# Turns of two token blocks, state products in one row, and diagonals on ScalarE, in a linear-attention kernel with two layers behind it

## The chip, the cores and the metric

The kernel runs on one core of a Trainium2 chip. The metric is the device time of that core in microseconds. Three timed runs and one profiled execution of the kernel before are at hand.

## The reference

First a linear attention with a decaying state, 4 sequences of 768 tokens, 8 heads of 48 channels; then two layers of width 384 - 2048 - 384 over the 3072 tokens:

```python
for t in range(S):
    cur = np.einsum('bhd,bhe->bhde', u[None] * kt, vt)
    y[:, :, t] = np.einsum('bhd,bhde->bhe', rt, state + cur)
    state = w[None, :, :, None] * state + np.einsum('bhd,bhe->bhde', kt, vt)
...
h = x @ w_in
sp = np.where(h > 20.0, h, np.log1p(np.exp(np.minimum(h, 20.0))))
x = (h * np.tanh(sp)) @ w_out
...
h = x @ w_in
P = a[0] + a[1] * h + a[2] * h2 + a[3] * h3
Q = 1.0 + np.abs(b[0]) * np.abs(h) + np.abs(b[1]) * h2
out = (P / (Q + 1e-06)) @ w_out
```

## The kernel before, in words

The attention is cut into 24 units. Unit U handles 128 tokens (chunk c of 6) of one sequence (b of 4), all 8 heads: c, b = divmod(U, 4). The function `unit` (L614) loads k, r (both transposed), and k, v in token order, scales them by powers of w, and makes one 128 by 128 score block for each head: row `sc` (L641). Two tiles `am` of four heads each are first written as diagonals (`diag`, L652: a mask times the column `dg`; on VectorE or GpSimd one instruction, L655, on ScalarE four, L658), then a predicated copy from PSUM puts the scores beside the diagonal (L663). `values` (L669) multiplies by the values (L673) and, where c is not 0, by the state of this sequence (L678), into one PSUM bank `pv`: for each pair of heads first the two products with values, then the two with the state. In the profile each such fp32 matmul is two records, so a unit has 16 records at L673 and 16 at L678. `kv` (L698) makes the chunk's own k-v products, which L707 to L712 add to the state. The result goes through SBUF and two DMAs (xr) and is split into a high and a low fp32r part, xh and xl (`split`, L476), 128 columns of the 512 of block c. xh and xl have two buffers each (L536), y and xr two, am four.

The two layers work on blocks of 512 tokens: block (l, c) is layer l, chunk c, and holds the four units of chunk c. A block is 16 steps, f = 0 to 15, one for each 128 of the 2048 inner columns. A step (`step`, L758) has nine matmuls g1 (L772: three times three products of high and low parts), the activation, a split of its result into gh and gl, and nine matmuls g2 (L848) that add into three PSUM banks `acc`, one buffer each (L742). In layer 0 the activation is one VectorE instruction (L787), four on ScalarE (L791), one on VectorE (L793); the split is a copy (mostly ScalarE) and a subtraction on VectorE (L797). At a block's end the three sums are scaled by -2, copied to SBUF and stored to `x2d` in HBM, where layer 1 reads them.

The list `steps` (L485 to L491) sets the order of the blocks. Block (0, 0) is done in half steps of 256 columns: half 0 of step i, then half 1 of step i - 2; half 0 needs units 0 and 1, half 1 units 2 and 3. All other blocks follow one by one in full steps of 512 columns. `weights(0, f)` (L724) loads one step's weights of layer 0 (768 KB) and turns the 64-bit numbers into two fp32r parts: one scaling on ScalarE or GpSimd, three integer instructions on VectorE (L64, L67, L71), a copy for the high part and a subtraction for the low part (L481).

The order on every engine is fixed at build time by a planner (`Plan.order`): each operation has one cost for each engine that may run it, a due time worked out back from the end, and a boost that makes it earlier. Units with c of 1 or more have boost AHEAD = 40 (L612). The cost of a VectorE option can carry an extra: `PV` = 0.0 (L467) for products of the units with c below 2 and the weights of layer 0, and 3.0 for all later ones. Before the first step, matmuls of zeros (L837, L841) fill gaps on TensorE; they open the accumulators of block (0, 0).

```python
    lag = 2
    steps = []
    for i in range(NF + lag):
        steps += [((0, 0), f, p) for f, p in ((i, 0), (i - lag, 1)) if 0 <= f < NF]
    for blk in blocks[1:]:
        steps += [(blk, f, None) for f in range(NF)]
```

Of the kernel before, what the change touches and what calls it, by code (L numbers as in the profile page):

```python
# [12 lines left out]
ALU = mybir.AluOpType  # L13
# [4 lines left out]
B, H, S, D = 4, 8, 768, 48  # L18
DM, DFF = 384, 2048
CH = 128  # L20
NC = S // CH
NF = DFF // 128
# [373 lines left out]
def tt(n):  # L396
    return 0.07 + 1.04e-3 * n
# [18 lines left out]
def fast_path(tc, nc, d):  # L416
    ctx, es1 = ExitStack(), ExitStack()
    V, A, G, T, SP = "V", "A", "G", "T", "S"
    eng = {V: nc.vector, A: nc.scalar, G: nc.gpsimd, T: nc.tensor, SP: nc.sync}
    pl = Plan()  # L420
# [26 lines left out]
    def fixed(p, name, shape, dt=F32):  # L447
        t = p.tile(shape, dt, name=name)
        b = Buf(None, lambda: t)
        return b  # L450

    def bc(x, n):
        return x[:, :, None].to_broadcast([x.shape[0], x.shape[1], n])

    def dma(dst, src, r=(), w=(), nbytes=196608, after=(), boost=0.0):

        return pl.add([(SP, 0.65 if nbytes == 98304 else 0.5)], lambda e: nc.sync.dma_start(out=dst(), in_=src()),
                      r=r, w=w, lat=0.757, after=after, move=nbytes / 3.6e5, boost=boost)
# [5 lines left out]
            return nc.gpsimd.tensor_scalar(out=out, in0=x, scalar1=1.0, scalar2=0.0, op0=ALU.mult, op1=ALU.add)  # L464
        return nc.vector.tensor_copy(out, x)

    PV = 0.0  # L467

    def hi_opts(n):
        return [(A, act(n)), (V, ts(n), True, 3.0), (G, pts(n))]  # L470
# [11 lines left out]
                      r=r + [w[0]], w=[w[1]], boost=boost, what=what)  # L482


    blocks = [(l, c) for l in range(2) for c in range(NC)]  # L485
    lag = 2
    steps = []
    for i in range(NF + lag):
        steps += [((0, 0), f, p) for f, p in ((i, 0), (i - lag, 1)) if 0 <= f < NF]
    for blk in blocks[1:]:  # L490
        steps += [(blk, f, None) for f in range(NF)]  # L491


    fin = cst.tile([1, 1], I32, name="fin")
# [14 lines left out]
    dmk = fixed(att, "dmk", [CH, CH])  # L509
# [99 lines left out]
                                              ps()[:, 0:192].rearrange("p (j e) -> p j e", j=4)),  # L609
                   r=[ps], w=[(P_t, i)])  # L610

    AHEAD = 40.0  # L612

    def unit(U):  # L614
        c, b = divmod(U, B)
        last = U >= NU - B
        bo = AHEAD if c else 0.0
        kraw, rraw, tkv, tr, dg = n_kraw(), n_rraw(), n_tkv(), n_tr(), n_dg()
        st = state[b]
        dma(kraw, lambda: d["kT"][c, b], boost=bo, w=[kraw], nbytes=262144)  # L620
# [30 lines left out]
        for i in range(2):  # L651
            def diag(e, i=i):  # L652
                dgi = dg().rearrange("p (j c) -> p c j", c=2)[:, i]
                if e != A:
                    return eng[e].tensor_tensor(out=am[i](), in0=dmk()[:, None, :].to_broadcast([CH, 4, CH]),  # L655
                                                in1=bc(dgi, CH), op=ALU.mult)
                for j in range(4):
                    x_ = nc.scalar.activation(out=am[i]()[:, j, :], in_=dmk(), func=AF.Copy, scale=dgi[:, j:j + 1])  # L658
                return x_
            pl.add([(G, 1.3), (V, tt(512), True, PV if c < 2 else 3.0), (A, 1.5)], diag, r=[dg, dmk], w=[am[i]], boost=bo)  # L660
        for i in range(2):
            pl.add([(V, tt(512))],
                   lambda e, i=i: nc.vector.copy_predicated(  # L663
# [3 lines left out]
        pv, y, xr = n_ps(), n_y(), n_xr()  # L667

        def values(e):  # L669
            for j in range(4):  # L670
                for i in range(2):
                    h = 2 * j + i
                    x_ = nc.tensor.matmul(pv()[64 * i:64 * i + D, j * CH:(j + 1) * CH],  # L673
                                          lhsT=tkv()[:, 384 + h * D:384 + (h + 1) * D], rhs=am[i]()[:, j, :],
                                          start=True, stop=(c == 0))
                for i in range(2 if c else 0):
                    rows = slice(64 * i, 64 * i + D)
                    x_ = nc.tensor.matmul(pv()[64 * i:64 * i + D, j * CH:(j + 1) * CH],  # L678
                                          lhsT=st()[rows, j * D:(j + 1) * D], rhs=rraw()[rows, j, :],
                                          start=False, stop=True)  # L680
            return x_
        pl.add([(T, 2.4 if c else 1.2)], values, r=[tkv, rraw] + ([st] if c else []) + am, w=[pv], boost=bo,
               rows=0.8)
        pl.add([(A, act(512, 0.052)), (V, tt(512))],
               lambda e: copy(e, y()[:, :, :CH], pv().rearrange("p (h t) -> p h t", h=4)), r=[pv], w=[y], boost=bo)
# [70 lines left out]


    def step(s, after):  # L758
        blk, f, half = steps[s]
        l, cb = blk  # L760
        n = 512 if half is None else 256
        col = 256 * (half or 0)
# [36 lines left out]
        else:  # L799
# [28 lines left out]
                   lambda e: nc.vector.scalar_tensor_tensor(out=g(), in0=g(), scalar=cf()[:, 0:1], in1=h(),  # L828
                                                            op0=ALU.add, op1=ALU.mult), r=[h, cf], w=[g])
            split(n, g, ghs, gls, g, (gh, gl))  # L830
        if f == 0 and not half:
            acc[blk] = [x() for x in n_acc]
            if half == 0:

                def zeros(e):
                    for a in acc[blk]:
                        x_ = nc.tensor.matmul(a(), lhsT=zer(), rhs=zer()[:, None, :].to_broadcast([CH, 4, CH]),  # L837
                                              start=True, stop=False)
                    return x_
                pl.filler = pl.add([(T, 0.64)], zeros, r=[zer], w=acc[blk])  # L840
                pl.fill = lambda e, a=acc[blk][0]: nc.tensor.matmul(  # L841
                    a(), lhsT=zer(), rhs=zer()[:, None, :].to_broadcast([CH, 4, CH]), start=False, stop=False)
        ac = acc[blk]

        def g2(e, ms=range(3)):
            for m in ms:
                for i, (a, x) in enumerate(((0, gh), (0, gl), (1, gh))):
                    x_ = nc.tensor.matmul(ac[m]()[:, col:col + n], lhsT=w()[:, a, 3 + m, :], rhs=x()[:, :n],  # L848
                                          start=(f == 0 and i == 0 and half is None),
                                          stop=(f == NF - 1 and i == 2 and half != 0))  # L850
            return x_
        last = s == len(steps) - 1
        if not last:
            follow(1, pl.add([(T, 9 * mm)], g2, r=rw + [gh, gl], w=[(a, 0) for a in ac], what="g2"), 18 * mm)
        if f == NF - 1 and half != 0:
            for m in range(3):
                if last:
                    y = pl.add([(T, 3 * mm)], lambda e, m=m: g2(e, [m]), r=rw + [gh, gl], w=[ac[m]], what="g2")
                    if m == 0:
                        follow(1, y, 18 * mm)  # L860
                o = n_o()

                def put(e, m=m, o=o):
                    if l:
                        return copy(e, o(), ac[m]())
                    if e == A:
                        return nc.scalar.activation(out=o(), in_=ac[m](), func=AF.Copy, scale=-2.0)
                    return nc.vector.tensor_scalar(out=o(), in0=ac[m](), scalar1=-2.0, scalar2=None, op0=ALU.mult)
                pl.add([(A, act(512, 0.052)), (V, tt(512))], put, r=[ac[m]], w=[o], boost=8.0)
                if l == 0:  # L870
                    dma(lambda m=m: x2d[cb]()[:, m, :], o, r=[o], w=[(x2d[cb], m)], nbytes=262144)
                else:
                    dma(lambda m=m: d["out"][cb, :, m, :], o, r=[o], nbytes=262144)
# [26 lines left out]
        weights(0, f)  # L900

    nu = 2
    for s, (blk, f, half) in enumerate(steps):
        need = 0 if blk[0] else B * (blk[1] + 1) if half is None else 2 * half + 2
        while nu < NU and nu < need:
            end = unit(nu)
            nu += 1
        if blk == (0, NC - 1) and f >= 1:
            weights(1, f - 1)
        if blk == (1, 0) and f == 0:  # L910
            weights(1, NF - 1)
        nxt = blocks.index(blk) + 1
        if f == 12 and half != 0 and nxt < len(blocks) and blocks[nxt][0] == 1:
            x2(blocks[nxt][1])
        step(s, [end])
    with tc.manual_schedule():
# [81 lines left out]
```

## Time and profile before

| what | value |
|---|---|
| timed runs | 979.3, 978.96, 970.26 us; median 978.96 |
| profiled execution, own time | 970.99 us |
| its span, first to last instruction | 969.3 us |
| mean granted clock of TensorE | 0.976 |
| busy: TensorE, VectorE, ScalarE, GpSimd | 930.1, 715.6, 727.3, 500.1 us |

The profile is one execution. Busy time of TensorE comes from records that overlap, since matmuls are pipelined: the distance from one start to the next tells more than a record's own length. A granted clock of 1.00 is 2.4 GHz, 0.50 is 1.2 GHz, and a stretch with both shows a mean.

### The profile page before, as it was taken

The page shows a single profiled execution, that of the slowest core. Times are in us where ns is not written, and L with a number is a line of the kernel's source. Part 1 is how long each engine was busy: PE and PEld are TensorE (multiplying, and loading weights), DVE is VectorE, ACT ScalarE, POOL GpSimd, SP SyncE. Part 2 cuts the span into 40 slices and gives each one's busy share as a digit, 9 for nine tenths or more (in the row PEclk, how much of TensorE's full clock was granted, in tenths as well). Part 3 has the DMA queues.
Part 4 walks back from the last instruction along what each step waited for, and adds up shares of the span by engine and source line. Part 5 has one row for each costly group of instructions (what it writes and reads, how often), then busy time and mean ns, then how long its engine had stood idle before and what let it go on. Part 6 is the DMA issues. An engine that isn't in the chain of part 4 may idle for free. (4 is left out here: it accounts for less than half of the span.)

```text
span 969.3 us, 14361 instructions
## 1 busy us (share of the span) xinstructions
PE 930.1 (96%) x5186; PEld 745.8 (77%) x5186; DVE 715.6 (74%) x1120; ACT 727.3 (75%) x1290; POOL 500.1 (52%) x441
## 2 busy tenths in 40 slices
PE   6798999999999999999999999999999999999995
PEld 4576788788778668767888878888888888888883
DVE  8999898874544544544458998888888788878883
ACT  2465776777677657666777998997988888979784
POOL 1345366420340560051037488786777786877673
PEclk7698999999999999999999999999999999999999
DMA  8765565300320350140025510010020100100001
GB/s 294 245 196 157 170 190 174 109 20 1 104 57 1 97 153 2 28 127 24 0 72 179 169 59 11 1 66 1 1 66 0 55 12 1 55 1 1 32 1 36
DMA packets 36848, 71.98 MB, mean 74 GB/s; under 512 B 4129, under 2 KB 16546, under 8 KB 36770
## 3 DMA queue, kind: packets, MB, share of 16 engines
q1 hardware_dynamic: 36770, 71.00, 23.2%
q8 instruction: 42, 0.69, 0.3%
q14 instruction: 36, 0.29, 0.1%
HBM read 56.83 MB, written 9.44 MB: 68 GB/s over the span
## 5 line engine op out<-in xcount | busy, mean ns | idle before, releaser
L848 PE MATMUL acc<-gh,w 128*128 128x512 f32 (+1 forms) x1248 | 391.5, 375 | 1.4 <-ACT gh L462 1.3
L772 PE MATMUL h<-xh,w 128*128 128x512 f32 (+1 forms) x1020 | 323.0, 377 | 11.5 <-DVE w L481 4.4
L791 ACT ACTIVATE e<-e 128x512 f32<-128x512 f32 (+1 forms) x448 | 250.7, 568 | 52.7 <-DVE e L787 44.2
L848 PEld LDWEIGHTS acc<-gh,w 128*128 128x128 f32 x1248 | 229.6, 188 | 45.8 <-ACT gh L462 2.8
L848 PE MATMUL acc<-gl,w 128*128 128x512 f32 (+1 forms) x624 | 233.4, 374 | 2.7 <-POOL gl L481 1.7
L772 PEld LDWEIGHTS h<-xh,w 128*128 128x128 f32 x1020 | 189.7, 191 | 50.4 <-DVE w L481 5.2
L772 PE MATMUL h<-xl,w 128*128 128x512 f32 (+1 forms) x510 | 190.2, 373 | 0.7 <-POOL xl L481 0.7
L481 POOL TENSOR_TENSOR gl<-yy,gh 128x512 fp32r<-128x512 f32 x96 | 125.4, 1308 | 46.5 <-ACT gh L462 31.5
L810 POOL TENSOR_TENSOR v<-v,x 128x512 f32<-128x512 f32 x96 | 124.9, 1304 | 32.5 <-ACT v L804 17.5
L848 PEld LDWEIGHTS acc<-gl,w 128*128 128x128 f32 x624 | 117.5, 188 | 24.8 <-POOL gl L481 2.7
L793 DVE SCALAR_TENSOR_TENSOR h<-e,h 128x512 f32<-128x512 f32 (+1 forms) x112 | 68.8, 615 | 81.9 <-ACT e L791 81.5
L772 PEld LDWEIGHTS h<-xl,w 128*128 128x128 f32 x510 | 97.7, 192 | 16.7 <-POOL xl L481 0.9
L787 DVE TENSOR_SCALAR e<-h 128x512 f32<-128x512 f32 (+1 forms) x112 | 68.4, 610 | 47.7 <-PE h L772 47.4
L462 ACT ACTIVATE gh<-h 128x512 fp32r<-128x512 f32 (+1 forms) x97 | 53.0, 547 | 59.0 <-DVE h L793 58.6
L812 ACT ACTIVATE x<-v,ceps 128x512 f32<-128x512 f32 x96 | 69.4, 723 | 17.5 <-POOL v L810 17.3
L797 DVE TENSOR_TENSOR gl<-h,gh 128x512 fp32r<-128x512 f32 (+1 forms) x112 | 68.4, 610 | 13.5 <-ACT gh L462 10.6
L804 ACT ACTIVATE v<-x,cf 128x512 f32<-128x512 f32 x96 | 78.2, 815 | 0.0
L772 PE MATMUL aps<-xh,w 128*128 128x512 f32 x228 | 76.3, 392 | 0.0
L712 POOL TENSOR_TENSOR st<-st,pw 128x192 f32<-128x192 f32 x16 | 9.2, 573 | 109.3 <-DVE st L710 109.3
L822 DVE SCALAR_TENSOR_TENSOR v<-v,ceps,h 128x512 f32<-128x512 f32 x58 | 43.2, 746 | 24.0 <-ACT h L820 23.8
L673 PE MATMUL aps<-am,tkv 128*48 128x128 f32 x384 | 45.2, 320 | 7.7 <-DVE am L663 7.7
L481 POOL TENSOR_TENSOR w<-wr,w 128x768 fp32r<-128x768 f32 x18 | 34.9, 1940 | 30.0 <-ACT w L462 29.4
(104 smaller groups left out, 1353.8 us busy)
## 6 DMA issues: line engine op xcount, KB each, us to landing
wr<-in_w SPq DMA_DIRECT2D x32, 768.0 KB, 4.4
tkv<-in_tkv SPq DMA_DIRECT2D x24, 384.0 KB, 3.5
kraw<-in_kT SPq DMA_DIRECT2D x24, 256.0 KB, 3.1
rraw<-in_rT SPq DMA_DIRECT2D x24, 256.0 KB, 2.9
tr<-in_tr SPq DMA_DIRECT2D x24, 192.0 KB, 2.4
xr<-y SPq DMA_DIRECT2D x48, 96.0 KB, 3.2
x<-o SPq DMA_DIRECT2D x18, 256.0 KB, 2.4
o<-x SPq DMA_DIRECT2D x18, 256.0 KB, 2.8
```

The source lines that it names most:

```text
L462: return nc.scalar.activation(out=out, in_=x, func=AF.Copy)
L481: lambda e: eng[e].tensor_tensor(out=lo(), in0=x(), in1=hi().bitcast(F32), op=ALU.subtract),
L673: x_ = nc.tensor.matmul(pv()[64 * i:64 * i + D, j * CH:(j + 1) * CH], lhsT=tkv()[:, 384 + h * D:384 + (h + 1) * D], rhs=am[i]()[:, j, :], ...
L772: x_ = nc.tensor.matmul(h()[:, :n], lhsT=w()[:, a, m, :], rhs=x()[:, m, col:col + n], start=(i == 0), stop=(i == 8))
L787: pl.add([(V, tt(n))], lambda e: nc.vector.tensor_scalar(out=es(), in0=hp(), scalar1=20.0, scalar2=None, op0=ALU.min), r=[h], w=[e_])
L791: lambda e, func=func, kw=kw: nc.scalar.activation(out=es(), in_=es(), func=func, **kw), w=[e_])
L793: lambda e: nc.vector.scalar_tensor_tensor(out=hp(), in0=es(), scalar=-0.5, in1=hp(), op0=ALU.add, op1=ALU.mult), r=[e_], w=[h])
L797: lambda e: nc.vector.tensor_tensor(out=gls(), in0=hp(), in1=ghs().bitcast(F32), op=ALU.subtract),
L804: lambda e: nc.scalar.activation(out=v(), in_=x(), func=AF.Identity, scale=cf()[:, 5:6], bias=cf()[:, 4:5]), r=[x, cf], w=[v])
L810: lambda e: eng[e].tensor_tensor(out=v(), in0=v(), in1=x(), op=ALU.mult), r=[x], w=[v])
L812: lambda e: nc.scalar.activation(out=x(), in_=v(), func=AF.Ln, bias=ceps()), r=[v, ceps], w=[x])
L848: x_ = nc.tensor.matmul(ac[m]()[:, col:col + n], lhsT=w()[:, a, 3 + m, :], rhs=x()[:, :n], start=(f == 0 and i == 0 and half is None), sto ...
```

## The change

1. Order of blocks. Blocks (0, 0) and (0, 1) take turns: (0, 0) f 0 to 7, (0, 1) f 0 to 7, (0, 0) f 8 to 15, (0, 1) f 8 to 15. Only the first six steps of the first turn are in halves, all of half 0 first. Since there is one set of accumulators, a turn's sums leave: the first turn's as at any block's end, and at the end of a block's second turn the stored sums are loaded again, added on VectorE (`if f0:`) and stored.
2. Units with c = 1 have boost 10 in place of 40; the others keep theirs.
3. `values`: all eight state products first, in one row, then all eight with the values.
4. `diag`: VectorE is no longer an option; ScalarE (cost 1.2 in place of 1.5) or GpSimd. PV is 0.3 in place of 0.0.

```diff
+    TURNS, HALVES = 2, 6
...
-    PV = 0.0
+    PV = 0.3
...
-    lag = 2
     steps = []
-    for i in range(NF + lag):
-        steps += [((0, 0), f, p) for f, p in ((i, 0), (i - lag, 1)) if 0 <= f < NF]
-    for blk in blocks[1:]:
-        steps += [(blk, f, None) for f in range(NF)]
+    for blk, f0, f1 in [(blocks[i % 2], NF // TURNS * (i // 2), NF // TURNS * (i // 2 + 1)) for i in range(2 * TURNS)] + \
+            [(blk, 0, NF) for blk in blocks[2:]]:
+        turn = [(f, None) for f in range(f0, f1)]
+        if not steps:
+            turn = [(f, i) for i in range(2) for f in range(HALVES)] + turn[HALVES:]
+        steps += [(blk, f, half, k == 0, k == len(turn) - 1, f0) for k, (f, half) in enumerate(turn)]
...
-    AHEAD = 40.0
+    AHEAD, AHEAD1 = 40.0, 10.0
...
-        bo = AHEAD if c else 0.0
+        bo = AHEAD if c > 1 else AHEAD1 if c else 0.0
...
-            pl.add([(G, 1.3), (V, tt(512), True, PV if c < 2 else 3.0), (A, 1.5)], diag, r=[dg, dmk], w=[am[i]], boost=bo)
+            pl.add([(A, 1.2), (G, 1.3)], diag, r=[dg, dmk], w=[am[i]], boost=bo)
...
         def values(e):
+            for j in range(4 if c else 0):
+                for i in range(2):
+                    rows = slice(64 * i, 64 * i + D)
+                    x_ = nc.tensor.matmul(pv()[64 * i:64 * i + D, j * CH:(j + 1) * CH],
+                                          lhsT=st()[rows, j * D:(j + 1) * D], rhs=rraw()[rows, j, :],
+                                          start=(j == 0), stop=False)
             for j in range(4):
                 for i in range(2):
                     h = 2 * j + i
                     x_ = nc.tensor.matmul(pv()[64 * i:64 * i + D, j * CH:(j + 1) * CH],
                                           lhsT=tkv()[:, 384 + h * D:384 + (h + 1) * D], rhs=am[i]()[:, j, :],
-                                          start=True, stop=(c == 0))
-                for i in range(2 if c else 0):
...
+                                          start=(j == 0 and c == 0), stop=(j == 3))
...
-        pl.add([(T, 2.4 if c else 1.2)], values, r=[tkv, rraw] + ([st] if c else []) + am, w=[pv], boost=bo,
+        pl.add([(T, 2.1 if c else 1.1)], values, r=[tkv, rraw] + ([st] if c else []) + am, w=[pv], boost=bo,
...
-        if f == NF - 1 and half != 0:
+        if final:
...
+                if f0:
+                    dma(o, lambda m=m: x2d[cb]()[:, m, :], r=[(x2d[cb], m)], w=[o], nbytes=262144, boost=20.0)
+                    pl.add([(V, tt(512) + 0.06)],
+                           lambda e, m=m, o=o: nc.vector.scalar_tensor_tensor(
+                               out=o(), in0=ac[m](), scalar=-2.0, in1=o(), op0=ALU.mult, op1=ALU.add),
+                           r=[ac[m]], w=[o], boost=8.0)
+                    dma(lambda m=m: x2d[cb]()[:, m, :], o, r=[o], w=[(x2d[cb], m)], nbytes=262144)
+                    continue
```

## Rows read from the trace of the kernel before

**Rows 1.** Stretches: busy us (records) of PE, PEld, DVE, ACT, POOL; clock, DMA share, GB/s.
```profile
0.00:37.84 37.84, 24.55 (x179) 18.67 (x179) 31.50 (x65) 11.70 (x17) 9.87 (x17) 0.73 0.87 292
37.84:100.00 62.16, 54.84 (x474) 42.50 (x474) 58.94 (x101) 38.12 (x94) 25.10 (x22) 0.83 0.59 176
100.00:176.75 76.75, 71.29 (x687) 59.25 (x686) 68.36 (x129) 54.73 (x137) 45.58 (x44) 1.00 0.55 173
176.75:251.50 74.75, 74.75 (x367) 61.86 (x365) 48.87 (x74) 56.27 (x96) 12.22 (x11) 1.00 0.11 33
...
500.00:961.70 461.70, 456.20 (x1995) 374.73 (x1993) 386.88 (x567) 395.78 (x650) 338.08 (x280) 1.00 0.12 41
```

**Rows 2.** The same view, line 673 on TensorE (products with values) alone.
```profile
0.00:37.84 37.84, 7.07 (x48) 0.73 0.87 292
37.84:100.00 62.16, 10.64 (x80) 0.83 0.59 176
100.00:176.75 76.75, 8.80 (x80) 1.00 0.55 173
```

**Rows 3.** Timeline of TensorE, one unit in steady state: start, us, instructions.
```profile
251.65 0.43 PE L673 MATMUL aps<-am,tkv 128*48 128x128 f32 x4
252.01 0.42 PE L678 MATMUL aps<-rraw,st 48*48 48x128 f32 x4
...
254.49 0.56 PE L698 MATMUL aps<-tkv 128*48 128x48 f32 x16
...
257.25 1.16 PE L641 MATMUL aps<-rraw,kraw 48*128 48x128 f32 x16
258.34 0.50 PE L848 MATMUL acc<-gh,w 128*128 128x512 f32 x1
```

**Rows 4.** Timeline of TensorE at half clock, values and state of a unit.
```profile
92.72 0.67 PE L673 MATMUL aps<-am,tkv 128*48 128x128 f32 x4
93.32 0.67 PE L678 MATMUL aps<-rraw,st 48*48 48x128 f32 x4
```

**Rows 5.** Timeline of weight loads at half clock, a unit without state.
```profile
46.49 1.51 PEld L673 LDWEIGHTS aps<-am,tkv 128*48 128x48 f32 x14 [0.40 <-issue]
```

**Rows 6.** Timeline of TensorE, half-width and full-width matmuls.
```profile
165.59 0.28 PE L772 MATMUL h<-xh,w 128*128 128x256 f32 x1
...
168.71 0.28 PE L772 MATMUL h<-xh,w 128*128 128x256 f32 x1
...
186.28 0.39 PE L848 MATMUL acc<-gh,w 128*128 128x512 f32 x1
...
188.32 0.39 PE L772 MATMUL h<-xh,w 128*128 128x512 f32 x1
```

**Rows 7.** Groups of VectorE's instructions, 0 to 179 us: count, busy us, mean ns.
```profile
L67 DVE SCALAR_TENSOR_TENSOR wr<-wr 128x768 int32<-128x768 int32 x17 | 19.0, 1115 | 0.0
...
L71 DVE SCALAR_TENSOR_TENSOR wr<-wr 128x768 int32<-128x768 int32 x16 | 16.6, 1037 | 0.0
L481 DVE TENSOR_TENSOR w<-wr,w 128x768 fp32r<-128x768 f32 x14 | 16.3, 1167 | 0.7 <-ACT w L462 0.7
...
L787 DVE TENSOR_SCALAR e<-h 128x256 f32<-128x256 f32 x32 | 13.3, 415 | 4.6 <-PE h L772 4.5
L64 DVE TENSOR_SCALAR wr<-wr 128x768 int32<-128x768 int32 x17 | 11.8, 704 | 0.0
L655 DVE TENSOR_TENSOR am<-dmk,dg 128x512 f32<-128x512 f32 x13 | 10.5, 823 | 0.1
```

**Rows 8.** Timeline of ScalarE: one diagonal tile, four instructions.
```profile
87.51 1.26 ACT L658 ACTIVATE am<-dmk,dg 128x128 f32<-128x128 f32 x4
```

**Rows 9.** Waits of TensorE, 0 to 175 us: total, times, longest.
```profile
PE aps L673 <- DVE am L663: 7.7, 3, 4.4
```

**Rows 10.** Groups by form, whole run: an evacuation on VectorE.
```profile
L868 DVE TENSOR_SCALAR o<-acc 128x512 f32<-128x512 f32 x7 | 4.8, 685 | 0.7 <-PE acc L848 0.7
```

**Rows 11.** Waits of all engines, whole run.
```profile
POOL xh L464 <- PE h L772: 39.6, 1, 39.6
```

More of the change, by code (lines that the diff above doesn't have):

```diff
@@ L674, in values @@
                                           lhsT=tkv()[:, 384 + h * D:384 + (h + 1) * D], rhs=am[i]()[:, j, :],
-                                          start=True, stop=(c == 0))
-                for i in range(2 if c else 0):
[L677 to L680, printed above, removed]
+                                          start=(j == 0 and c == 0), stop=(j == 3))
             return x_
-        pl.add([(T, 2.4 if c else 1.2)], values, r=[tkv, rraw] + ([st] if c else []) + am, w=[pv], boost=bo,
+        pl.add([(T, 2.1 if c else 1.1)], values, r=[tkv, rraw] + ([st] if c else []) + am, w=[pv], boost=bo,
                rows=0.8)
@@ L758, in step @@
     def step(s, after):
-        blk, f, half = steps[s]
+        blk, f, half, first, final, f0 = steps[s]
         l, cb = blk
@@ L830, in step, with zeros @@
             split(n, g, ghs, gls, g, (gh, gl))
-        if f == 0 and not half:
+        if first:
             acc[blk] = [x() for x in n_acc]
-            if half == 0:
-                def zeros(e):
-                    for a in acc[blk]:
+            if s == 0:
+                def zeros(e, first=acc[blk]):
+                    for a in first:
                         x_ = nc.tensor.matmul(a(), lhsT=zer(), rhs=zer()[:, None, :].to_broadcast([CH, 4, CH]),
@@ L848, in g2 @@
                     x_ = nc.tensor.matmul(ac[m]()[:, col:col + n], lhsT=w()[:, a, 3 + m, :], rhs=x()[:, :n],
-                                          start=(f == 0 and i == 0 and half is None),
-                                          stop=(f == NF - 1 and i == 2 and half != 0))
+                                          start=(first and i == 0 and s > 0), stop=(final and i == 2))
             return x_
@@ L902, in fast_path @@
     nu = 2
-    for s, (blk, f, half) in enumerate(steps):
+    for s, (blk, f, half, *_) in enumerate(steps):
         need = 0 if blk[0] else B * (blk[1] + 1) if half is None else 2 * half + 2
@@ L912, in fast_path @@
         nxt = blocks.index(blk) + 1
-        if f == 12 and half != 0 and nxt < len(blocks) and blocks[nxt][0] == 1:
+        if f == 12 and nxt < len(blocks) and blocks[nxt][0] == 1:
             x2(blocks[nxt][1])
```

## The prediction

> **What bounds the kernel now.** I read the share of each engine by stretch first [rows 1]. From 176.75 to 251.5 us TensorE is busy in all of the time at full granted clock, and from 500 to 961.7 in 456.2 of 461.7 us: there the time is TensorE's own work, and only less of that work, or an earlier start of it, shortens the run. Before 176.75 us it is otherwise. VectorE is busy for 31.50 of 37.84, 58.94 of 62.16 and 68.36 of 76.75 us, ScalarE and GpSimd for clearly less, and TensorE has gaps and a granted clock of 0.73 and 0.83 in the first two stretches (a mean between its two levels). The one wait of TensorE that stands out there is the products with the values waiting for am from VectorE [rows 9].
>
> How much is lost before 186.28 us, where the first 512-wide g2 starts? Spacing comes from the timeline [rows 6]: a 256-wide matmul takes (168.71 - 165.59) / 26 = 0.120 us, a 512-wide one (188.32 - 186.28) / 9 = 0.2267 us. Until 186.28 TensorE has done block (0,0), 576 x 0.120 = 69.1 us, and three g1 of block (0,1), 27 x 0.2267 = 6.1. It has also done the values of 13 units (48 + 80 + 80 = 208 records, 16 for each unit [rows 2]), nine of them with a state. A unit at full clock costs [rows 3]: 254.49 - 251.65 = 2.84 us for values and state, 258.34 - 257.25 = 1.09 for scores, and the k-v products' row takes 0.56. Values without state I take as one row like the scores, 1.1. That is 13 x 1.09 + 9 x 2.84 + 4 x 1.1 + 12 x 0.56 = 50.9 us, and some 38 changes between kinds of rows, estimated at 0.11 us, add 4. Sum 130.1, so 56.2 us of the first 186.28 are lost, 30 of them before the first g1 at 37.84. That is what the order of the first blocks can give back; nearly nothing can be given back later.
>
> The values of 13 units by 176.75 us also say that all of c = 1 and c = 2 were made while block (0,0), which needs only units 0 to 3, was still running. VectorE spent its scarce time on work not yet due.
>
> **The change, part by part. Rows of products.** Now a unit's values and state alternate in groups of four records, a group every 0.354 us (252.01 - 251.65) [rows 3], though the records inside a group follow closely: the row of 16 score records with the same halves of the array takes 1.09, change to the next kind included. At half clock the trace has both forms: the alternating groups are 93.32 - 92.72 = 0.60 us apart [rows 4], and 14 weight loads of values alone take 1.51 us, with an estimated 0.2 for the last one's own length, so about 0.10 each and 0.40 for four [rows 5]. So the alternation, not the arithmetic, costs 0.2 us a group there. At full clock the two new rows cost at most 2 x 1.09 = 2.18 us (the score row loads 128 columns, these load 48), and at least 2 x 16 x 0.05 + 2 x 0.13 = 1.9, half the half-clock spacing plus two changes. The saving is 0.66 to 0.94 us, in no case shown below zero; I take 0.66, the nearest row. 20 units have a state: 13.2 us, up to 19. All of them run where TensorE is or becomes the bound, so nothing hides the saving.
>
> The Trainium skill, page "TensorE: Matmul & The Clock Gate", section "Wait — 56ns, not 53.3ns?", says that without hardware decode a matmul occupies the sequencer for about 62 ns; two rows would then cost 2 x 16 x 0.062 + 0.26 = 2.24 us, and the saving would be 12 us, an estimate from that page. The k-v row here speaks against that floor, 16 records in 0.56 us, 0.035 each [rows 3].
>
> **Fewer half-width steps.** 32 half steps become 12 and ten full steps: 10 x 18 x (2 x 0.120 - 0.2267) = 2.4 us saved.
>
> **Turns.** The first turn (block (0,0), f 0 to 7) needs units 0 to 3 and eight weights in place of sixteen; units with c = 1 have a boost of 10 in place of 40. I sum VectorE, the binding engine. A weight costs 0.70 + 1.12 + 1.04 + 1.17 = 4.0 us on it [rows 7], a half step 3 x 0.415 = 1.25, a full step at 0.69 each 2.07 (the width of the evacuation in [rows 10]). All 158.8 us of VectorE up to 176.75 [rows 1] less 63.7 for weights, 43 for the steps (3 x 13.3 and some copies), 10.5 for diagonals and an estimated 6 for constants leave 35.6 for 13 units, 2.7 each; with the tail of contention I take 3. First turn: 4 x 3 + 8 x 4.0 + 12 x 1.25 + 2 x 2.07 + 6 = 69 us, and VectorE idled 9.6 us in the first 100, so it ends at about 79. TensorE's work by then is 12 x 2.16 + 2 x 4.08 + 4 x 2.7 + 1.5 = 46.4, so 33 us are lost. Second turn: TensorE 8 x 4.08 + 4 units of 3.8 = 48 us, VectorE 8 x 2.07 + 4 x 3 = 29: TensorE binds, and VectorE has 19 us for the weights of the third turn. Third: VectorE 8 x 6.1 = 49 less those 19, TensorE 33 to 48. So it binds no more; I allow 5 us for places where order is worse than the sum. Loss 38 in place of 56.2: 18 us saved, between 0 (nothing of it comes) and 28 (TensorE busy from 37.84 on).
>
> **Diagonals.** Thirteen leave VectorE, 10.5 us [rows 7], for ScalarE at 4 x 0.316 = 1.26 us each [rows 8] or GpSimd. This is in the sum of the turns (units at 3 us, without them). ScalarE has room: 38.12 of 62.16 us and 54.73 of 76.75 busy [rows 1]. Without that room it would cost TensorE's wait for am again, 1.26 - 0.8 a tile, 16 x 0.5 = 8 us at most over the first eight units. PV 0.3 moves some early products to GpSimd in the same way, where half of the time is free; I take 0, between -3 and +3.
>
> The Trainium skill, page "ScalarE: Activation LUTs", section "Rules for kernel authors", tells to keep plain multiplies on VectorE. The rows agree as to the single instruction (1.26 against 0.82); by that rule the chain of each unit grows and those 8 us come on top, giving about 948 in the profile. VectorE's load of 95% decides against it, I think.
>
> **Turnover.** Two more turn ends: three sums leave for HBM, come back and are added on VectorE, 0.69 us each [rows 10]. The loads are early and the next turn's g1 (2.04 us each, three banks) cover the evacuation; I take 1 us for each added end, 2 in all, 0 to 6.
>
> **Sum.** -13.2 - 2.4 - 18 + 2 = -31.6 us, from the profiled execution's 970.99 us (span 969.3) to 939.4. The three other times known are 970.26, 978.96 and 979.3, so the median shown lies 8 us above the profiled execution; the middle of all four is some 4 us above it, and I set the forecast at 944.
>
> **Rivals.** (1) Only TensorE's own savings come. VectorE stays the bound through all four turns because the same weights, units and steps are still due, or the third turn starves for weights 8 to 15. For: its total hardly falls. Against: blocks (0,0) and (0,1) with twelve units need 6 + 16 x 4 + 12 x 1.25 + 26 x 2.07 + 12 x 3 = 175 us of it, and TensorE needs some 207 by then. Gain 13.2 + 2.4 - 2: 957 in the profile, 961 as forecast. (2) More comes: first g1 earlier, a denser first turn, rows at 1.9 us. -19 - 2.4 - 26 + 2: 926 to 930. (3) The rows don't become cheaper, as both add into the same bank and each product must wait for the one before. Against it the half-clock row [rows 5]. Then -20 + 2: 953 to 957. (4) Slower: x has two buffers, so the x of block (0,2) can be written only after the last g1 of the third turn. Before there was a whole block of 65 us behind that point, now half a block, 33 us. For: GpSimd stood 39.6 us before such a write [rows 11]. y and xr have two buffers as well, so if all four units queue behind that point, they come two by two; I estimate 23 us for a pair, from the 37.84 us that the first pair took with constants and first loads. 2 x 23 = 46 us of chain, and were none of it covered, 939 + 46 = 985. It decides against the change from 32 us of stall on. Against: two units can be ready up to the write, and 33 us cover the other pair.
>
> **How the numbers follow.** Forecast 0.62 (its own range 930 to 955), rival (1) 0.18, (2) 0.11, (3) 0.05, (4) 0.04. Low 922 takes in rival (2); high 964 takes in (1) and its 8 us of scatter; about 0.15 is left out. About 1% is what can be told from no change. Faster by over 1%: forecast, (2), (3) and two thirds of (1), 0.90; within 1%: the rest of (1), 0.06; slower: 0.04.
>
> **What would show it.** Right: values and state of a unit as two rows, scores-like, 2.2 us or less to the next row; TensorE busy throughout from about 80 us; no diagonals on VectorE; c = 2 units after 115 us. Wrong: groups as far apart as now; waits of g1 for w after 115 us; waits of g1 for xh or xl at the start of block (0,2); TensorE waiting for accumulators at turn ends.

## The result, and the profile after

| | before | after |
|---|---|---|
| median, us (four runs each) | 974.97 | 946.13 |
| range, us | 970.26 to 979.3 | 943.59 to 946.39 |
| profiled execution, its span, us | 970.99, 969.3 | 946.39, 944.4 |
| mean granted clock | 0.976 | 0.977 |
| first sums leave, us (before: block (0,0); after: its first turn) | 183.8 | 117.5 |
| first Abs of layer 1 on ScalarE, us | 560.6 | 537.2 |

The ratio is 0.9699, 95% interval 0.9637 to 0.9762: faster by 3%. The forecast of 944 is 2 us off. By profiled executions, which is how the sum was made, it is 946.39 against 939.4: 24.6 us gained in place of 31.6, at nearly the same mean granted clock. By medians it is 28.8 us, since the profile of before was one of its faster executions and that of after the slowest of its four. Of the 24.6, 23.4 are there when layer 1 begins, so nearly the whole effect arises ahead of it.

The sum was 7 us too high and its parts were further off than that, as the following views show. First the timeline of TensorE after, at a unit of the first turn and at the end of the second turn; the columns are as in [rows 3], L679 is the row with the state, L685 the one with the values, L705 the k-v row, L779 is g1 and L855 g2.

```profile
69.95 1.08 PE L679 MATMUL aps<-rraw,st 48*48 48x128 f32 x16
70.96 1.08 PE L685 MATMUL aps<-am,tkv 128*48 128x128 f32 x16
71.87 0.53 PE L705 MATMUL aps<-tkv 128*48 128x48 f32 x16
...
155.39 0.39 PE L855 MATMUL acc<-gh,w 128*128 128x512 f32 x1
155.71 1.08 PE L679 MATMUL aps<-rraw,st 48*48 48x128 f32 x16
156.72 1.08 PE L685 MATMUL aps<-am,tkv 128*48 128x128 f32 x16
157.73 0.50 PE L779 MATMUL h<-xh,w 128*128 128x512 f32 x1
```

A unit's two rows now take 71.87 - 69.95 = 1.92 us up to the k-v row, where they took 2.84 [rows 3]: 0.92 saved. The sixteen records of values take 0.91, 0.057 each on the average. The last four rows are the end of the second turn: from the last g2 to the first g1 of the third turn TensorE does only the two rows of a unit, and nothing waits for an accumulator.

The stretches of the kernel after (columns as in [rows 1]; cut at the first g1, inside the first turn, and near the ends of the turns):

```profile
0.00:33.70 33.70, 23.60 (x166) 16.89 (x166) 27.68 (x56) 13.39 (x25) 11.01 (x20) 0.80 0.87 304
33.70:60.00 26.30, 17.90 (x128) 15.29 (x128) 25.73 (x42) 16.25 (x39) 16.40 (x11) 0.63 0.60 188
60.00:87.00 27.00, 25.58 (x300) 23.12 (x301) 20.26 (x43) 16.27 (x42) 14.83 (x15) 0.92 0.68 209
87.00:117.50 30.50, 26.50 (x181) 22.20 (x182) 28.80 (x39) 21.11 (x47) 21.55 (x18) 0.97 0.35 109
117.50:155.10 37.60, 37.60 (x209) 30.26 (x208) 34.72 (x51) 30.21 (x49) 15.54 (x12) 0.98 0.54 180
155.10:197.50 42.40, 42.00 (x299) 33.43 (x299) 32.37 (x48) 29.57 (x55) 27.11 (x27) 1.00 0.48 151
197.50:238.50 41.00, 41.00 (x256) 33.01 (x256) 28.89 (x45) 28.81 (x51) 10.41 (x11) 1.00 0.26 81
```

The same view for the state rows (L679) alone; records, 16 to a unit:

```profile
60.00:87.00 27.00, 4.56 (x64) 3.53 (x64) 0.92 0.68 209
87.00:117.50 30.50, 0.00 (x0) 0.00 (x0) 0.97 0.35 109
117.50:155.10 37.60, 1.08 (x16) 0.82 (x16) 0.98 0.54 180
155.10:197.50 42.40, 3.23 (x48) 2.47 (x48) 1.00 0.48 151
```

From 117.5 us on TensorE has no gap worth naming (37.60 of 37.60, 42.00 of 42.40, 41.00 of 41.00), which before was so from 176.75 on [rows 1]. But the first turn ends at 117.5 and not at about 79, and the state rows say what is in it: all four units of c = 1 (64 records) stand between 60 and 87 us, where the prediction had them in the second turn.

Waits of the kernel after, all engines (total, times, longest):

```profile
POOL xh L466 <- PE h L779: 47.1, 2, 39.7
...
PE aps L685 <- DVE am L668: 9.1, 5, 3.1
```

GpSimd still stands 39.7 us before a write of xh, as in [rows 11], but g1 never waits for xh or xl: from 117.5 to 238.5 us the waits of TensorE add up to 0.4 us. The wait for am is still there.

Groups of the whole run: the diagonals, and the addition of stored sums at turn ends:

```profile
L663 ACT ACTIVATE am<-dmk,dg 128x128 f32<-128x128 f32 x100 | 31.8, 392 | 24.0 <-DVE dg L638 24.0
L660 POOL TENSOR_TENSOR am<-dmk,dg 128x512 f32<-128x512 f32 x23 | 24.9, 1085 | 10.9 <-DVE dg L638 10.6
L871 DVE SCALAR_TENSOR_TENSOR o<-acc,o 128x512 f32<-128x512 f32 x6 | 3.8, 683 | 0.0
```

Of 48 diagonal tiles 25 are ScalarE's and 23 GpSimd's; VectorE has none. The added sums cost VectorE 3.8 us, 0.683 each, the size of the evacuation in [rows 10].

### The profile page after: what moved, and what is told of

The parts are those of the page before. It is cut to its first block, busy times and chain, and to the rows that moved or that the text cites. A ratio compares the mean times of both kernels' runs of the same rounds, so it can differ in the third digit from the quotient of the medians.

```text
span 944.4 us, 13963 instructions
## 1 busy us (share of the span) xinstructions
PE 907.2 (96%) x5009; PEld 739.6 (78%) x5009; DVE 705.2 (75%) x1072; ACT 723.2 (77%) x1256; POOL 527.7 (56%) x464
## 5 line engine op out<-in xcount | busy, mean ns | idle before, releaser
L855 PE MATMUL acc<-gh,w 128*128 128x512 f32 (+1 forms) x1188 | 391.3, 388 | 1.9 <-DVE gh L467 1.0
L779 PE MATMUL h<-xh,w 128*128 128x512 f32 (+1 forms) x960 | 318.3, 389 | 6.5 <-DVE w L483 3.5
L798 ACT ACTIVATE e<-e 128x512 f32<-128x512 f32 (+1 forms) x408 | 245.7, 606 | 42.5 <-DVE e L794 34.5
L855 PEld LDWEIGHTS acc<-gh,w 128*128 128x128 f32 x1188 | 223.3, 190 | 49.2 <-ACT gh L464 2.2
L855 PE MATMUL acc<-gl,w 128*128 128x512 f32 (+1 forms) x594 | 229.7, 387 | 5.5 <-DVE gl L804 2.9
L779 PEld LDWEIGHTS h<-xh,w 128*128 128x128 f32 x960 | 181.5, 191 | 45.8 <-DVE w L483 4.8
L779 PE MATMUL h<-xl,w 128*128 128x512 f32 (+1 forms) x480 | 184.7, 385 | 0.0
L855 PEld LDWEIGHTS acc<-gl,w 128*128 128x128 f32 x594 | 112.7, 190 | 29.3 <-DVE gl L804 3.5
L779 PEld LDWEIGHTS h<-xl,w 128*128 128x128 f32 x480 | 92.1, 192 | 16.8
L779 PE MATMUL aps<-xh,w 128*128 128x512 f32 x228 | 75.7, 389 | 0.0
L663 ACT ACTIVATE am<-dmk,dg 128x128 f32<-128x128 f32 x100 | 31.8, 392 | 24.0 <-DVE dg L638 24.0
L779 PEld LDWEIGHTS aps<-xh,w 128*128 128x128 f32 x228 | 42.8, 188 | 8.9
```

What stands on the lines that cost most here:

```text
L779: x_ = nc.tensor.matmul(h()[:, :n], lhsT=w()[:, a, m, :], rhs=x()[:, m, col:col + n], start=(i == 0), stop=(i == 8))
L798: lambda e, func=func, kw=kw: nc.scalar.activation(out=es(), in_=es(), func=func, **kw), w=[e_])
```

## The experiments

The kernel before was timed again beside these runs, 27 times on three chips: medians 973.92 (with e1 to e4), 975.55 (e5 to e8) and 974.43 us (e9 to e12). All ratios are to the runs on the same chip. A difference to the kernel after is given by medians and, where it matters, by ratios; the two can differ by 4 us.

**e1: rows alone.** The kernel before with the new `values`, the planner's costs as they were.

```diff
+            for j in range(4 if c else 0):
+                for i in range(2):
...
+                                          start=(j == 0), stop=False)
...
-                                          start=True, stop=(c == 0))
-                for i in range(2 if c else 0):
...
+                                          start=(j == 0 and c == 0), stop=(j == 3))
```

> The kernel before, with the products of a unit in the two rows of the change and nothing else; the order on every engine and the planner's costs stay. In the profile after, a row of 16 records takes 0.91 to 1.01 us, so a unit's two rows take 1.92 in place of 2.84 us and 20 units save 18.4. Theory A (TensorE's own time counts wherever it is saved): 18 us faster, ratio 0.981. Theory B (before 176.75 us VectorE binds, so that the 9 units with a state that lie there give nothing): 11 x 0.92 = 10 us faster, ratio 0.990. If the rows bring nothing but with the new order: 1.00.

Median 958.57 (956.36 to 960.9), ratio 0.9859 [0.9807, 0.9911]: 13.7 us of 974 by the ratio and 15.4 by medians, between the two theories. Timeline of ScalarE, when the sums of blocks (0,0) and (0,1) leave. Before:

```profile
183.79 1.22 ACT L867 ACTIVATE o<-acc 128x512 f32<-128x512 f32 x2
...
251.31 1.07 ACT L867 ACTIVATE o<-acc 128x512 f32<-128x512 f32 x2
```

and in e1:

```profile
182.30 1.08 ACT L869 ACTIVATE o<-acc 128x512 f32<-128x512 f32 x2
...
248.98 1.06 ACT L869 ACTIVATE o<-acc 128x512 f32<-128x512 f32 x2
```

Nine units with a state are done by 176.75 us [rows 2], so 9 x 0.92 = 8.3 us of TensorE's work are gone, but at 183.8 only 1.5 us of it have come and at 251.3 only 2.3. The other 11.5 of the 13.8 us between the spans (969.3 and 955.5) come later, where 11 units x 0.92 = 10.1 lie. In this pair of profiles the saving comes in full where TensorE is always busy and hardly at all before.

**e2: all but the rows.** The kernel after with the old `values`; the planner's costs as they are after.

```diff
-            for j in range(4 if c else 0):
...
+                                          start=True, stop=(c == 0))
+                for i in range(2 if c else 0):
...
```

> The kernel after, with values and state alternating again as before, order on every engine unchanged. Theory A: 18 us slower than the kernel after, some 965, ratio to before 0.989. Theory B: the four units with a state that lie in the first turn cost nothing, 16 x 0.92 = 15 us slower than after, 961, ratio 0.985.

956.37 (954.78 to 960.02), ratio 0.9844 [0.9792, 0.9895]: 10 us more than after by medians, 14 by ratios. The rows are worth about as much here as alone.

**e3: turns alone.** The kernel before with the new order of steps, halves and boosts, and the stored sums; rows, diagonals and PV as before.

```diff
+    TURNS, HALVES = 2, 6
...
+    for blk, f0, f1 in [(blocks[i % 2], NF // TURNS * (i // 2), NF // TURNS * (i // 2 + 1)) for i in range(2 * TURNS)] + \
...
-    AHEAD = 40.0
+    AHEAD, AHEAD1 = 40.0, 10.0
...
```

> The kernel before with the turns, the halves of the first six steps and the boost of 10, but with the old products, old diagonals and PV 0. By the sum of the prediction (18 saved at the start, 2.4 for the half steps, 2 lost at turn ends): 18 us faster, ratio 0.981. If the units 4 to 7 must be ready before the second turn begins, so that VectorE has them to do in the first turn as well, the start saves little: 2 to 6 us faster, ratio 0.994 to 0.998.

964.12 (961.98 to 968.61, ten runs), ratio 0.9901 [0.9874, 0.9928]: 9.6 us, with the half steps' 2.4 in it: between the two expectations. The first turn's sums leave at 120.0 us.

**e4: all but the turns.** The kernel after with the old list of steps.

```diff
-    for blk, f0, f1 in [(blocks[i % 2], NF // TURNS * (i // 2), NF // TURNS * (i // 2 + 1)) for i in range(2 * TURNS)] + \
...
+    lag = 2
+    for i in range(NF + lag):
...
```

> The kernel after with the old order of blocks (block (0,0) whole, in half steps, lag of two), all else as after: new products, diagonals off VectorE, PV 0.3, boost 10 for c = 1. By the prediction's sum the turns are worth 18 us and it comes to some 962, ratio 0.987. If the turns give little by themselves: 948 to 953, ratio 0.972 to 0.977.

952.7 (950.81 to 955.49), ratio 0.9795 [0.9744, 0.9847]: 6.6 us more than after by medians, 9.4 by ratios. So turns with fewer half steps bring 7 to 10 us either way, and not the forecast's 18 + 2.4 - 2, some 18.

**e5: units 4 to 7 left out.**

```diff
-            end = unit(nu)
+            if nu // B != 1:
+                end = unit(nu)
...
+        if blk == (0, 1):
+            xt[blk] = xt[(0, 0)]
```

> The kernel after without the four units of c = 1: they are left out (loads, products, x), and block (0,1) reads the x of block (0,0); all else is planned as after. It tests the sum for the first turn. In the kernel after the first turn's sums leave at 117.5 us and units 4 to 7 run before that. Theory P (the prediction's costs for the first turn are right, only these four units were put in the wrong turn): without them the first turn's sums leave at 79 to 88 us. Theory Q (the costs themselves are too small, since GpSimd's instructions slow VectorE's): not before 100 us.

One run: 919.98 us. The work of four units is missing from the whole run, so only the length of its first turn is compared. The first turn's sums leave at 97.2 us, between what the two theories expect: these four units, with what follows from them, cost it 20.3 us, and the other 18 between 79 and 97 have another reason. Groups of VectorE from 0 to 97.2 us in e5:

```profile
L67 DVE SCALAR_TENSOR_TENSOR wr<-wr 128x768 int32<-128x768 int32 x11 | 12.4, 1124 | 0.0
L71 DVE SCALAR_TENSOR_TENSOR wr<-wr 128x768 int32<-128x768 int32 x11 | 11.5, 1043 | 0.0
...
L668 DVE COPY_PREDICATED am<-msk,aps 128x512 f32<-128x512 uint32 x12 | 8.3, 725 | 0.2 <-ACT am L663 0.2
```

The turn needs eight weights and four units. VectorE has worked on eleven weights, and twelve copies at two a unit are six units. Part of VectorE's time up to 97 us is thus work ahead of its due time. Whether that work holds up work already due is not shown here.

**e6: diagonals and PV as before.**

```diff
-    PV = 0.3
+    PV = 0.0
...
-            pl.add([(A, 1.2), (G, 1.3)], diag, r=[dg, dmk], w=[am[i]], boost=bo)
+            pl.add([(G, 1.3), (V, tt(512), True, PV if c < 2 else 3.0), (A, 1.5)], diag, r=[dg, dmk], w=[am[i]], boost=bo)
```

> The kernel after with the diagonals' old choice of engine (GpSimd, VectorE, ScalarE) and PV 0.0. If VectorE binds the first turn, some eleven diagonals at 0.8 us come back to it: 5 to 9 us slower than after, ratio to before 0.975 to 0.979. If what leaves VectorE is given back because GpSimd's own instructions hold VectorE up: within 2 us of after, 0.968 to 0.972.

947.77 (946.81 to 950.17), ratio 0.9718 [0.9685, 0.9752], the first turn's end at 117.5 us as after. The parts 4 and PV of the change are worth 0 to 2 us.

**e11: diagonals on ScalarE alone.**

```diff
-            pl.add([(A, 1.2), (G, 1.3)], diag, r=[dg, dmk], w=[am[i]], boost=bo)
+            pl.add([(A, 1.2)], diag, r=[dg, dmk], w=[am[i]], boost=bo)
```

> The kernel after with ScalarE as the only engine for diagonals. In the first 117 us of the kernel after GpSimd is busy for 63.8 us, and a weight's three integer instructions take 3.4 us on VectorE; in the turns with old diagonals and PV 0 it is 37.3 and 2.6 us. If GpSimd's work holds VectorE up, nine tiles of 1.05 us less of it shorten the first turn by 2 to 4 us: 0.966 to 0.968. If the diagonals wait behind the activations on ScalarE: 3 us slower or more, 0.973.

946.31 (945.09 to 947.78), ratio 0.973 [0.9669, 0.9791]: by the median as after, by the ratio 3 us slower, with intervals that overlap: no difference that can be told. First turn's end 113.1 us.

Where the 10.5 us taken off VectorE went is seen by comparing the groups of after, e3 and e6 up to 117.5 us. With the diagonals off VectorE (after; GpSimd is busy for 63.79 us of this stretch):

```profile
L67 DVE SCALAR_TENSOR_TENSOR wr<-wr 128x768 int32<-128x768 int32 x10 | 12.3, 1225 | 0.0
...
L71 DVE SCALAR_TENSOR_TENSOR wr<-wr 128x768 int32<-128x768 int32 x9 | 11.0, 1225 | 0.0
L64 DVE TENSOR_SCALAR wr<-wr 128x768 int32<-128x768 int32 x10 | 9.3, 939 | 0.0
...
L638 DVE TENSOR_REDUCE dg<-tr 128x8 f32<-128x384 f32 x10 | 5.5, 546 | 0.7 <-POOL tr L635 0.7
```

With fourteen of them on VectorE (e3; GpSimd is busy for 37.65 us):

```profile
L67 DVE SCALAR_TENSOR_TENSOR wr<-wr 128x768 int32<-128x768 int32 x11 | 11.3, 1050 | 0.0
L71 DVE SCALAR_TENSOR_TENSOR wr<-wr 128x768 int32<-128x768 int32 x11 | 11.3, 1025 | 0.0
...
L660 DVE TENSOR_TENSOR am<-dmk,dg 128x512 f32<-128x512 f32 x14 | 9.9, 738 | 0.1
...
L64 DVE TENSOR_SCALAR wr<-wr 128x768 int32<-128x768 int32 x12 | 6.4, 553 | 0.0
...
L638 DVE TENSOR_REDUCE dg<-tr 128x8 f32<-128x384 f32 x9 | 4.9, 540 | 0.0
```

The three integer instructions of a weight take 1.225 + 1.225 + 0.939 = 3.39 us after and 1.050 + 1.025 + 0.553 = 2.63 in e3, the same instructions on the same shapes. Ten weights make that 7.6 us. In e6, which differs from after by the diagonals and PV alone, they take 1.119 + 1.071 + 0.750 = 2.94 (GpSimd 42.99), so there it is 4.5 us of the 10.3 that its fourteen diagonals cost VectorE.

What makes these instructions longer can be read from the timelines of VectorE and GpSimd. In the kernel after:

```profile
27.02 1.73 POOL L633 TENSOR_TENSOR tr<-tr,ub 128x384 f32<-128x384 f32 x1
27.80 1.37 DVE L64 TENSOR_SCALAR wr<-wr 128x768 int32<-128x768 int32 x1
...
48.51 0.56 DVE L64 TENSOR_SCALAR wr<-wr 128x768 int32<-128x768 int32 x1
48.73 2.40 POOL L653 TENSOR_TENSOR tkv<-tkv,P_t 128x384 f32<-128x384 f32 x1 [3.28 <-PE h L779]
```

The first L64 begins while a GpSimd instruction runs and ends 0.42 us after it (29.17 against 28.75). The second begins 0.22 us before one and takes 0.56; now the GpSimd instruction is the long one, 2.40 us where the shortest of its kind take 0.99. It is the same in all fourteen traces: the 301 L64 that begin outside GpSimd's instructions take 0.54 to 0.58 us, and 137 of the 147 that begin inside one end 0.41 to 0.53 us after it. So these instructions of VectorE wait for one of GpSimd that has begun before them. GpSimd's busy time in sum does not tell how often that happens: in e12 it is 66.66 us up to 117.5 us, more than in after, and a weight's three instructions take 2.80 us.

The Trainium skill, page "SBUF — State Buffer", section "Who interferes with whom", says that VectorE and GpSimd share a pair of ports which one instruction holds to its end, and that a reduction is never touched by it. The rows agree with both: the L64 above waits to the other's end, and the reduction in L638 takes 0.546 and 0.540 us in the two views. In the fourteen traces no reduction into dg takes over 0.57 us, beside GpSimd's instructions or without them.

The other 6 us of e6's diagonals became idle time of VectorE. The stretch up to 117.5 us of after and of e6, in which the first turn ends at the same time:

```profile
0.00:117.50 117.50, 93.58 (x769) 77.50 (x770) 102.46 (x178) 67.02 (x152) 63.79 (x63) 0.83 0.63 206
0.00:117.50 117.50, 96.08 (x775) 80.37 (x776) 108.79 (x198) 61.51 (x128) 42.99 (x47) 0.81 0.64 210
```

VectorE is busy 102.46 us in after and 108.79 in e6. So the end of the first turn does not go by the sum of VectorE's work alone; which chain of waits sets it is open.

**e7: the second turn begins in halves too**, so that units 6 and 7 are due later.

```diff
-        if not steps:
-            turn = [(f, i) for i in range(2) for f in range(HALVES)] + turn[HALVES:]
+        if len(steps) < 20:
+            k = HALVES if not steps else 4
+            turn = [(f, i) for i in range(2) for f in range(k)] + turn[k:]
...
-        need = 0 if blk[0] else B * (blk[1] + 1) if half is None else 2 * half + 2
+        need = 0 if blk[0] else B * (blk[1] + 1) if half is None else B * blk[1] + 2 * half + 2
```

> The kernel after with the first four steps of the second turn, block (0,1) f 0 to 3, in halves as well: half 0 needs only units 4 and 5, units 6 and 7 are due four half steps and 9 us later. If the due time of units 4 to 7 sets the first turn's length, its sums leave 5 to 10 us earlier than 117.5 and the run is 2 to 6 us faster than after (four half steps cost 1 us), ratio 0.964 to 0.968. If the weights set it: no earlier, 1 to 2 us slower.

946.75 (942.58 to 948.98), ratio 0.9689 [0.9648, 0.973]. The first turn ends at 113.9 us, 3.6 earlier, less than the 5 to 10 expected if the due time of all four units set its end, and nothing of it is left in the time.

**e8 and e12: other boosts for c = 1**, 40 and 0 in place of 10.

```diff
-    AHEAD, AHEAD1 = 40.0, 10.0
+    AHEAD, AHEAD1 = 40.0, 40.0
```

> The kernel after with boost 40 for the units of c = 1, as before. If the second turn needs these units ready at its start whatever the boost, the boost matters little: within 3 us of after, 0.967 to 0.973. If the lower boost is what relieved the start, as the prediction had it: 8 us slower or more, 0.978.

> The kernel after with boost 0 for the units of c = 1, so that they come as late as their due time allows. With 10 and 40 the first turn's sums left at 117.5 and 117.8 us. If the due time at the start of the second turn decides, again 115 to 119 us and within 3 us of after: 0.967 to 0.973. If a lower boost frees VectorE for the weights: the first turn ends 5 us earlier or more, 0.965 or less.

e8: 942.47 (941.75 to 945.96), ratio 0.9657 [0.9628, 0.9686], first turn's end 117.4. e12: 940.26 (936.58 to 942.96), ratio 0.9661 [0.9594, 0.9728], first turn's end 111.0. Both medians lie 4 to 6 us below after's, one with the boost up, one with it down, and the intervals of the ratios overlap after's. So the boost of 10 is no term of the gain that these runs can tell. In e12 the first turn does end 6.5 us earlier, as its second expectation has it for a VectorE freed for the weights, and its four times all lie below those of after.

**e9 and e10: matmuls of zeros for longer.** The planner fills TensorE's gaps with zeros up to 80 us of its own time, not 30; e10 has a boost of 40 as well.

```diff
-    FILL = 30.0
+    FILL = 80.0
```

> The kernel after with the matmuls of zeros allowed in gaps up to planned 80 us in place of 30, all other orders as after. In the kernel after the granted clock is 0.63 from 33.7 to 60 us and 0.92 from 60 to 87, behind gaps of TensorE. If VectorE sets the pace of the first turn, a faster TensorE there gives 0 to 2 us: ratio 0.968 to 0.970. If half clock is itself on the path (47 half-width matmuls of layer 0 and one unit at twice the time, some 5 us, and the clock of the next stretch), 4 to 8 us faster than after: 0.962 to 0.966.

> The same with boost 40 for the units of c = 1, the fastest of the four before this. If both help a little and add: 0.960 to 0.964, faster than both kernels. If the difference of the boost was within the scatter: as the run with the zeros alone.

e9: 941.53 (940.74 to 942.91), ratio 0.968 [0.962, 0.9741]; e10: 940.95 (940.76 to 943.26), ratio 0.9677 [0.9616, 0.9739]. Stretches of e9, to be held against the second and third row of after above:

```profile
33.70:60.00 26.30, 23.12 (x166) 19.15 (x166) 26.20 (x42) 15.74 (x42) 15.73 (x11) 0.96 0.58 188
60.00:87.00 27.00, 26.40 (x316) 23.62 (x315) 24.20 (x51) 18.52 (x46) 12.72 (x12) 1.00 0.67 213
```

The granted clock is 0.96 in place of 0.63 from 33.7 to 60 us, nearly all of it at 2.4 GHz, and VectorE does 51 instructions in place of 43 in the next stretch. The first turn ends at 112.3 us. The time of e9 is 4.6 us below after's by medians, with ranges that don't overlap, and 1.9 by ratios, whose intervals do; with the boost of 40 in both (e10 against e8) the longer zeros bring 1.5 by medians and nothing by ratios. So of the lost time before 117.5 us at most some 5 us go with this change, and the planner orders the other work around the zeros too, so clock and order are not told apart here. e9, e10 and e12, at 940 to 942 us, have the lowest medians. They are faster than before without doubt; against after, which was not timed beside them, the ratios leave it open.

## Why the prediction was right, and where it was not

**The time.** 946.1 against 944, in the forecast's own range of 930 to 955. That it came within 2 us is in part luck. The sum promised 31.6 us and the profiles show 24.6: the turns brought 12.5 us less than their term, while the rows brought 5 more and the turn ends cost 2 less. The rest of the closeness comes from the step from 939.4 to 944, an allowance for medians above the profiled time, as they were before; after, the profiled execution was the slowest of the four and the median 0.3 us below it.

**Rows of products: the mechanism right, the size low.** The unit saves 0.92 us, not 0.66; the upper bound of 0.94 was the good one. The bounds came from half the half-clock spacing, and that nearly held (0.057 us a record against 0.05). "All of them run where TensorE is or becomes the bound" failed for the units ahead of 117.5 us: four of twenty stand there, and e1 shows that the saving hardly arrives where TensorE has gaps. TensorE has 20 x 0.92 = 18.4 us less to do; 16 x 0.92 = 14.7 us should come as time, beside 13.2 predicted and 10 to 15 measured in e1 and e2. The floor of 62 ns for a matmul without hardware decode on the Trainium skill's page "TensorE: Matmul & The Clock Gate" (section "Wait — 56ns, not 53.3ns?") doesn't show if each record is one: 0.057 us a record in the row of values, 0.035 in the k-v row. Counted by matmuls of the program, two records each, it is 0.114 and 0.07, and no run tells which count the page's figure is for. On the cost of alternating, the Trainium skill's page "TensorEngine Tiling (Array Packing)", section "Key Properties", says that a change of tiling mode drains TensorE; 2.84 us with eight alternating groups against 1.92 in two rows agrees, though no run tells a drain from another cost of the change.

**Turns: the step that failed.** The forecast had a loss of 38 us in place of 56.2. By the prediction's own count of work, TensorE had done by 117.5 us: 12 x 2.16 + 2 x 4.08 = 34.1 for the steps, 4 x 2.75 = 11.0 for units 0 to 3, 4 x 3.57 = 14.3 for units 4 to 7, 1.1 for another row of scores, 2.2 for changes of kind and 4.1 for two early g1, together 66.8. So 50.7 us were lost there. Under 1 us was lost after, up to the end of the third turn. The turns saved 56.2 - 50.7 = 5.5 us, not 18. With the half steps' 2.4 that is 7.9, and e3 and e4 measure 7 to 10.

The sentence "Second turn: TensorE 8 x 4.08 + 4 units of 3.8 = 48 us" is wrong. A full-width g1 of block (0,1) reads all 512 columns, so units 4 to 7 are due at the start of the second turn, not in its course, and belong to the first turn's VectorE. All four stand before 87 us in the rows of the state. The first turn's VectorE sum of 69 us was in fact 102.46. Ten weights at 12.3 + 11.0 + 9.3 and 8.4 for subtractions make 41 in place of 32. The steps have 24 in place of 19, and 37.5 in place of 18 remain for constants and eight and a half units instead of four. Its idle time was 15.0 instead of 9.6. These differences, 33.5 + 5.4, make up the way from 79 to 117.5 us, as busy and idle time always add up to the whole; they say where the time went and not yet why. e5 shows the cause of 20 of them: units 4 to 7. For the other 18 the cause stays open. VectorE's longer instructions, its work ahead of the due time (even e5 shows it) and half clock are in them, and e6 shows that VectorE's sum of work doesn't set the end by itself. The statement "TensorE busy throughout from about 80 us" fell with it: it is so from 117.5.

What the prediction said of the turns behind this one held: TensorE binds in the second, third and fourth, and g1 doesn't wait for w after 117.5 us. The 5 us allowed there weren't needed.

**Diagonals and PV.** They left VectorE, as expected, and the chains of the units did not grow by the 8 us of the rival rule: the wait for am is 9.1 us against 7.7 [rows 9]. But the 10.5 us did not come as time either. e6 puts the part at 2 us or less, and e11 shows no gain from moving all of them to ScalarE. GpSimd took 23 tiles of the 48, and VectorE's own instructions became longer behind GpSimd's, which no term of the prediction had; the rest became idle time of VectorE. The advice of the Trainium skill, page "ScalarE: Activation LUTs", section "Rules for kernel authors", to leave multiplies to VectorE is thus neither borne out nor refuted here.

**Turnover.** Priced at 2 us, it shows none: the 2.3 us between g2 and g1 at 155 us are a unit's rows.

**Sum by what the profiles show.** The 50.7 us lost count units 4 to 7 at their new price, so the rows of all twenty units stand beside them: -18.4 - 2.4 - 5.5 + 0 = -26.3, beside 24.6 between the two profiled executions. With 14.7 for the rows the four units' 3.7 us go to the turns, 9.2, and the sum is the same. The 1.7 us between them are within what the counts above, some of them estimates, can carry.

**Rivals.** (1), only TensorE's savings: nearest to the truth in its reason, a VectorE busy for 102 of the first 117.5 us, but only in the first of four turns, and 946.4 lies well under its 957. (2), more: its rows came, its turns did not. (3), rows no cheaper: refuted by the timeline. (4), slower through two x buffers: GpSimd stood 39.7 us before the write, and no engine that matters waited for it.

## What to carry to other kernels

Matmuls that use the array in the same way should stand in one row: here two rows in place of eight alternating groups saved a third of the time of a unit's products with values and state, and only where TensorE is always busy did that become run time. When an order of work is changed to relieve an engine, put each piece in the stretch in which it falls due for the first instruction that reads any of it, not the stretch that uses it up. Work that moves from VectorE to GpSimd is not free for VectorE: look at the mean length of VectorE's other instructions after the move, and at which of the two engines begins first.

## What the runs showed of the hardware that was not expected

VectorE's 128x768 integer scaling (L64) took 0.54 to 0.58 us in all 301 cases in which it began with no GpSimd instruction running. Begun inside one, it mostly ended 0.41 to 0.53 us after that one's end, and took up to 1.68 us. Its mean up to 117.5 us was 0.553 us in e3, 0.750 in e6 and 0.939 in after.

The granted clock differs between runs of the same kernel, and the time goes with it: of the 27 runs of before beside the experiments, the nine at a mean clock of 0.965 to 0.969 took 975.6 to 979.2 us, the two at 0.979 took 969.3 and 969.4, and the five at 0.976 lie between 968.3 and 976.2. A comparison of a few us between two orders can therefore be a comparison of clocks. In e8 it may be one: its runs at 0.976, 0.980, 0.981 and 0.984 took 945.96, 942.65, 941.75 and 942.29 us, the first of them as long as after at 0.977. In e12 the clock of the whole run is not the reason: 939.73 us at 0.978.
